# Sparse chunk attention and a gated MLP on one core: six head pairs score mask and data in one 128-row contraction, early bounds in three terms, and a new written order

## The chip, the cores and the metric

The kernel runs on one core of a Trainium2 chip. The metric is the device time of one launch in microseconds (us). A few runs are taken and the median is compared. A separate profiled execution gives the rows that are quoted below; PE is the matrix engine, PEld its weight loads, DVE the vector engine, ACT the scalar engine, POOL the general engine and SP the engine that only issues DMAs here.

## The reference, cut to what matters

There are 4 batches and 8 heads of 768 positions by 64. Keys lie in 24 chunks of 32. Each query keeps the six chunks with the largest upper bound of its score, and attends to these under the causal mask. The output of all heads, 512 wide, goes through a gated MLP with a mixing matrix over positions.

```python
ub = sum(max(q * k_min, q * k_max))          # per query and chunk; -1e9 where the chunk lies ahead
top = argsort(ub)[-6:]
scores = where(selected & causal, q @ k.T / 8, -1e9)
x = softmax(scores) @ v                       # heads side by side: 768 x 512 per batch
h = relu(x @ w_in);  u, w = h[:, :512], h[:, 512:]
w_n = (w - mean(w)) / sqrt(var(w) + 1e-6)
out = (u * (w_spatial @ w_n + b)) @ w_out
```

## The kernel before, in words

**Work items.** Two heads form a pair; there are 16 pairs, four for each batch. Pairs 0 to 3 (batch 0) are worked in two halves of 384 positions, named 0a, 0b and so on; pairs 4 to 15 are whole. Each pair passes through `load`, `prep` and `attend`, and after the four pairs of a batch `mlp` runs. The kernel is not scheduled by its loops. Each call of `op(name, costs, function, reads, writes)` makes a work item, and a table, `ORDER`, lists all the items in one written sequence, with a letter for the engine (P for PE, D, A, G for POOL, S for SP) and digits for the buffers taken. `replay` (L115 on) gives engines and buffers by this table, and each engine runs its items in that order. The numbers in `op` served the search for the table and play no part on the chip.

**prep** (L490 to L628). Queries and keys are cast to 16 bits (`c_k`, `c_q`). For pairs 0 to 9 PE transposes them (`t_k`, `t_q`, L516) and ACT or DVE evicts the result (`e_k`, `e_q`); for pairs 10 to 15 one DMA transpose does both (`x_kq`, L524). DVE reduces each key chunk to maximum and minimum (`kmm`, L530), with the minimum negated, and small copies place them (`km`). `rq0` and `rq1` (L541 to L550) make relu(q) and relu(-q). Two matmuls for each tile of 128 queries (`ub`, L558) then give the bound, relu(q) times maximum plus relu(-q) times negated minimum. `ubm` (L567) adds the causal mask of the diagonal on DVE. `max` (L576, L581) finds the largest eight, `grd` (L590) makes a guard column, `sel` (L602, L605) a 0/1 matrix of chunks that are not selected, three PE transposes (`tsel`, L616) turn it, and `es` evicts it.

**attend** (L630 to L762). For whole pairs the scores lie in three groups of two PSUM tiles, each with seven blocks of 128 by 128 for each head in three or four strips (`WHOLE`). A group is two sets of matmuls. In the first (L658) each strip contracts the 64 rows of one head, and the two heads use the two halves of the array. In the second (L671) each strip contracts 32 rows of `expand` (a chunk's column spread over its 32 keys, times -30000) with the turned selection, and adds the mask. ACT takes the exponential (`exp`, L693), POOL zeroes the upper triangle of diagonal blocks (`tri`, L704), PE multiplies by the values (`av`, L727), DVE normalizes (`rec`, `nrm`), and a DMA or PE transpose (`xx`, `tx`) puts the result where the MLP reads it.

**mlp** (L764 on). For each of six tiles: `v` and `u` projections (L776), relu (`rv`, `ru`, L783, L785), statistics (`bn`, `ag`), `ln` and `rs` for the reciprocal deviation, `vn` (L808) to normalize, `s` (the mixing matrix, L826), `g` (L830), a transpose `xg` (L847), `o` (L855), its eviction `eo`, and the store `so` (L860).

**Order around the change.** PE begins with 22 matmuls on zeros (`w0` to `w3`, L424), 13 of them ahead of the first transpose. SP issues every DMA; an issue that waits holds all that follow it.

Of the kernel before, what the change touches and what calls it, by code (L numbers as in the profile page):

```python
# [14 lines left out]
P = 128  # L15
# [7 lines left out]
XBAR = 1300.0  # L23
# [11 lines left out]
def t_pool(n):  # L35
    return n * 0.9 + 85.0
# [107 lines left out]
RINGS = {"hst": 9, "st": 8, "kqT": 6, "kq16": 2, "x16": 2, "x16d": 2, "e": 7, "vraw": 6, "selT": 5}  # L144
# [17 lines left out]
t_k3aP:3 tsel1aP:2 e_k3aD:3 es1aD:1 kmm0_3aD:0 t_k0bP:0 t_q3aP:1 ub2aP:3 ubm2aD: kmm1_3aD: t_q0bP:2 e_q3aA: max2aD:0
rq1_3aD:1 sel2aD:1 rq0_3aD: e_k0bA: kmm1_0bD:1 preset_vt4G: km1_3aG:4 grd2aG: c_k1bG:2 preset_vt1G: c_q2bG:1 c_v1aG:5
e_q0bA: km0_3aA: sc1a_0P:01 exp1a_01A:1 exp1a_00A: av0aP:1 tsel2aP:0 ub3aP:2 t_k1bP:3 es2aD:2 rq0_1bD:0 ubm3aD:
kmm0_0bD: rq0_0bA:1 rq1_0bA: e_k1bA: max3aD:1 rec0aD:0 km0_0bA: sel3aD:1 nrm0aD:0 kmm0_1bD:2 c_k2bG:0 grd3aG: km1_0bG:
sc2a_0P:10 tsel3aP:0 av1aP:3 ub0bP:2 t_q2bP:1 es3aD:3 rec1aD:1 ubm0bD: kmm1_1bD: max0bD:0 nrm1aD:1 t_k2bP:0 sel0bD:1
c_q3bG:3 c_v2aG:4 km1_1bG: c_q4G:2 grd0bG: c_wv2G:0 c_k3bG:1 c_v3aG:1 exp2a_01A:2 exp2a_00A: rq1_1bA: e_q2bA: km0_1bA:
e_k2bA: sc3a_0P:01 t_q3bP:1 e_q3bD: tx0aP:3 ub1bP:0 tsel0bP:2 es0bD:4 ubm1bD: max1bD:1 tx1aP:1 av2aP:2 rec2aD:2
sel1bD:1 nrm2aD:0 kmm0_2bD:0 exp3a_00A:3 exp3a_01A: sc0b_0P:01 av3aP:0 rec3aD:0 tx2aP:2 nrm3aD:1 ex2aD:0 rq1_3bD:1
rq0_2bA:0 ex0aA: ex1aA: exp0b_01A:4 exp0b_00A: t_k3bP:3 grd1bG: t_q4P:1 tsel1bP:0 tx3aP:2 e_k3bA: ex3aD: c_v0bD:  # L170
c_wv0G: es1bD:0 c_wu2D:0 kmm1_2bD: kmm0_3bD:1 c_wv1G: c_wv3G: ld_wu1S:7 ld_wu3S:1 ld_wo3S:2 ld_ws4S:4 ld_k4S:5
ld_ws3S:6 sc0b_1P:10 exp0b_10A:5 exp0b_11A: e_q4A:4 rq0_3bD: v0_0P:2 v0_2P:3 km0_2bG: c_wu0A: tri0b_00G: sc1b_0P:10
rq1_2bD: rv0_0D:0 exp1b_00A:6 exp1b_01A: c_wu3G: tri0b_10G: km1_2bG: kmm1_3bD: ub2bP:0 ubm2bD: rq1_4D:0 max2bD:0
grd2bD:1 km1_3bG: c_ws4G:0 av0bP:2 rec0bD:1 v0_1P:1 bn0_0D:0 sel2bD: c_wu1G: nrm0bD:0 km0_3bG: c_k4G:3 c_ws3G:1
rv0_2A:1 rv0_1A:2 sc1b_1P:10 ub3bP:3 tsel2bP:0 ubm3bD: es2bD:1 exp1b_10A:0 exp1b_11A: bn0_2D:1 max3bD:1 sel3bD:1
u0_0P:1 t_k4P:2 tws3P:0 ld_ws2S:0 tri1b_00G: c_ws2G:2 grd3bG: ld_k5S:1 ld_v2bS:4 c_v2bD: c_k5G:3 tri1b_10G: ld_q5S:3
ld_k6S:4 ld_v1bS:5 ld_wo2S:7 sc2b_0P:10 e_k4A: ru0_0A:0 exp2b_00A:1 exp2b_01A: ews3D:0 tws2P:3 tsel3bP:2 es3bD:2
bn0_1D:2 kmm1_4D:2 ag0_0D:0 kmm0_4D: rq0_4D: t_k5P:1 u0_2P:0 tx0bP:2 sc2b_1P:10 e_k5A:5 ld_ws5S:5 u0_1P:1 ex0bA:
exp2b_10A:2 exp2b_11A: ld_ws1S:6 ld_k7S:0 c_v1bG: av1bP:2 tri2b_00G: km1_4G:1 epsG:0 km0_4G: tri2b_10G: ag0_2D:
kmm1_5D:0 ru0_1A:1 ews2D: rec1bD:2 kmm0_5D: nrm1bD:1 ru0_2A:2 c_k6G:1 c_q5G:2 sc3b_0P:10 exp3b_00A:3 exp3b_01A: ub4P:3  # L180
tws4P:1 t_q5P:0 av2bP:2 ubm4D: max4D:0 ag0_1D: sel4D:0 rec2bD:0 nrm2bD:0 sc3b_1P:10 ld_v5S:1 ld_v3bS:7 ld_q7S:4
km0_5A:0 km1_5G: e_q5A: exp3b_10A:4 exp3b_11A: c_ws5G:3 grd4G: c_k7G:0 c_ws1G:2 tri3b_00G: tri3b_10G: tx1bP:3 tx2bP:0
ews4D: ex1bD: ex2bD: rq0_5D:1 tws5P:2 tsel4P:1 rq1_5D: es4D:3 tws1P:3 t_k7P:0 ews5D: c_q7D:3 ews1D: e_k7A:0 sc4_0P:10
exp4_01A:5 exp4_00A: ub5P:1 c_wo3G: c_v3bG: av3bP:2 ubm5D: max5D:1 rec3bD:1 nrm3bD:1 sel5D:0 t_k6P:0 grd5G: ld_q6S:3
c_q6G:2 ld_k8S:5 ld_ws0S:0 c_ws0G:0 ld_v4S:6 c_v4G:0 ln0_0A:0 e_k6A:1 rs0_0A: sc4_1P:01 exp4_11A:0 exp4_10A: tx3bP:3
t_q7P:2 t_q6P:0 ex3bD: tsel5P:1 v0_3P:3 sc4_2P:10 e_q6A: rv0_3A:3 e_q7A: exp4_20A:6 exp4_21A: v0_4P:0 u0_3P:3 v0_5P:2
ru0_3A:3 rv0_4A:4 rv0_5A:5 kmm0_7D:1 es5D:4 kmm1_6D:2 vn0_2D:0 bn0_3D:0 vn0_1D:1 kmm0_6D: rq1_6D:0 rq1_7D:1 ag0_3D:1
kmm1_7D: bn0_4D:1 bn0_5D:2 rq0_6D: sc5_0P:10 exp5_00A:1 exp5_01A: c_v5G:5 tri4_00G: ag0_4D: tri4_20G: tri4_10G:
km1_7G:3 km1_6G:4 ld_q8S:2 c_k8G:1 tws0P:1 u0_4P:3 av4_0P:0 av4_1P:2 ld_wo0S:4 c_wo0G: c_q8G:3 ews0A: ld_k9S:3 bcolS:0
ld_k10S:0 c_k9G:2 ld_k11S:6 km0_6G: ld_q12S:1 ld_q10S:5 ag0_5D: vn0_0D:2 ln0_1A:1 rec4_0D:2 nrm4_0D:0 rec4_1D:0  # L190
nrm4_1D: ru0_4A:4 rs0_1A: sc5_1P:10 t_k8P:1 t_q8P:0 ub6P:3 u0_5P:2 exp5_11A:2 exp5_10A: sc5_2P:01 e_k8A:2 vn0_5D:3
vn0_4D:4 c_wo2D: ubm6D: vn0_3D:5 ru0_5A:5 e_q8A: exp5_20A:3 exp5_21A: max6D:0 c_q12G:0 km0_7G: tri5_10G: grd6G:0
c_k10G:1 c_q10G: sel6D: kmm1_8D:0 s0_0P:1 tsel6P:2 s0_1P:3 rq0_7A: es6D:0 kmm0_8D: g0_1D:0 g0_0D: rq1_8D:0 sc6_0P:01
ub7P:0 t_k9P:2 s0_2P:3 exp6_01A:4 exp6_00A: sc6_1P:10 km0_8G:1 preset_snb0G: ld_v6S:4 ld_k12S:2 ubm7D: max7D:1 grd7G:0
tri5_20G: rq0_8D: exp6_11A:0 exp6_10A: km1_8A: g0_2D:1 ld_wo1S:3 x_kq10S:3 e_k9D:4 c_wo1A: sel7D: rq0_10D:1 kmm0_10D:2
tri5_00G: s0_3P:1 av5_1P:3 tsel7P:2 es7A:1 ld_q9S:7 c_q9G:0 c_k11G:1 g0_3D: kmm1_9D:1 sc6_2P:01 exp6_21A:5 exp6_20A:
xg0_1S:0 ld_v8S:1 ld_v9S:0 s0_4P:0 o0_1P:2 eo0_1A:0 sc7_0P:10 exp7_01A:6 preset_km2G: kmm1_10D: rec5_1D:1 nrm5_1D:
# [68 lines left out]
def kernel(  # L266
# [645 lines left out]
```

## Time and profile before

| | us |
|---|---|
| median of 3 runs | 205.67 (204.78 to 205.95) |
| profiled execution, its own time | 205.87 |
| its span in the trace | 204.0 |
| mean granted clock of PE | 0.988 |
| busy: PE, DVE, ACT, POOL | 190.9, 164.5, 145.8, 80.1 |

The span runs from the first to the last instruction of the trace; the profiled execution's own time is 1.87 us longer. Rows of a timeline begin with the start and the length in us. A matmul's length in such a row contains the way through the array, which overlaps the next one; the price of a set of matmuls is therefore read from its start to the start of what follows.

### The profile page before, as it was taken

The page shows a single profiled execution, that of the slowest core. Times are in us where ns is not written, and L with a number is a line of the kernel's source. Part 1 is how long each engine was busy: PE and PEld are TensorE (multiplying, and loading weights), DVE is VectorE, ACT ScalarE, POOL GpSimd, SP SyncE. Part 2 cuts the span into 40 slices and gives each one's busy share as a digit, 9 for nine tenths or more (in the row PEclk, how much of TensorE's full clock was granted, in tenths as well). Part 3 has the DMA queues.
Part 4 walks back from the last instruction along what each step waited for, and adds up shares of the span by engine and source line. Part 5 has one row for each costly group of instructions (what it writes and reads, how often), then busy time and mean ns, then how long its engine had stood idle before and what let it go on. Part 6 is the DMA issues. An engine that isn't in the chain of part 4 may idle for free.

```text
span 204.0 us, 5938 instructions
## 1 busy us (share of the span) xinstructions
PE 190.9 (94%) x2282; PEld 103.3 (51%) x2282; DVE 164.5 (81%) x523; ACT 145.8 (71%) x232; POOL 80.1 (39%) x167
## 2 busy tenths in 40 slices
PE   7899989999998999798999999999999999999991
PEld 2456646576564455454355554544455456444440
DVE  2699999999999999798499896979998418894352
ACT  4689989999999498746797986687884673344221
POOL 5377848785795455631304642101451121000000
PEclk9969999999999999999999999999999999999998
DMA  5999999989999599699999869999200570701844
GB/s 167 278 249 292 287 359 280 319 223 310 275 208 238 92 224 236 142 145 263 236 213 230 155 78 262 148 261 224 40 0 3 132 154 5 204 2 51 206 156 157
DMA packets 86989, 38.28 MB, mean 188 GB/s; under 512 B 74416, under 2 KB 81584, under 8 KB 86960
## 3 DMA queue, kind: packets, MB, share of 16 engines
q1 hardware_dynamic: 86960, 37.89, 79.4%
q8 instruction: 18, 0.29, 0.6%
q14 instruction: 11, 0.09, 0.1%
HBM read 24.38 MB, written 6.29 MB: 150 GB/s over the span
## 4 chain that ended last, share of the span: by engine, by line
PE 59%; DVE 20%; DMA 7%; POOL 7%; issue 4%; ACT 2%; POOLq 0%; DVEq 0%; ACTq 0%
PE gen L776 16%; PE gen L826 11%; PE gen L855 7%; PE gen L727 7%; PE sc L658 6%; DVE kmm L530 5%; PE sc L671 4%; DMA st<-in_q_dram 3%; POOL n L306 3%; DMA late<-late 2%; PE sc L424 2%; DMA out_dram<-late 2%; DVE max L581 2%; DVE vn L808 2%; PE gen L616 2%
## 5 line engine op out<-in xcount | busy, mean ns | idle before, releaser
L693 ACT ACTIVATE e<-sc 128x768 f16<-128x768 f32 (+1 forms) x96 | 83.2, 917 | 23.3 <-PE sc L671 22.4
L704 POOL TENSOR_SCALAR_AFFINE_SELECT e<-e 128x512 f16<-128x512 f16 (+1 forms) x44 | 28.6, 662 | 31.8 <-ACT e L693 30.0
L826 PE MATMUL gen<-vn,wsT 128*128 128x512 f16 x144 | 34.4, 380 | 0.0
L530 DVE TENSOR_REDUCE kmm<-kqT 128x24 f16<-128x768 f16 (+1 forms) x40 | 30.7, 780 | 0.4 <-ACT kqT L304 0.2
L658 PE MATMUL sc<-kqT 64*128 64x128 f16 (+2 forms) x344 | 27.4, 272 | 0.3 <-ACT e L693 0.3
L727 PE MATMUL gen<-vt,e 128*128 128x65 f16 x672 | 24.8, 193 | 0.5 <-DVE selT L306 0.3
L727 PEld LDWEIGHTS <-e 128*128 128x128 f16 x672 | 23.0, 97 | 4.5 <-issue 1.6
L855 PE MATMUL gen<-w_out,late 128*128 128x512 f16 x96 | 23.7, 379 | 1.2 <-DMA late<-late 1.2
L830 DVE SCALAR_TENSOR_TENSOR late<-gen,bcol,u 128x512 f16<-128x512 f32 x24 | 17.7, 745 | 7.8 <-PE gen L826 7.8
L826 PEld LDWEIGHTS <-wsT 128*128 128x128 f16 x144 | 12.9, 98 | 15.7 <-issue 2.6
L671 PE MATMUL sc<-selT,expand 32*128 32x128 f16 (+2 forms) x344 | 19.0, 273 | 0.2 <-DVE selT L306 0.2
L658 PEld LDWEIGHTS <-kqT 64*128 64x128 f16 x344 | 11.8, 94 | 13.5 <-issue 9.8
L304 ACT ACTIVATE kqT<-gen 128x384 f16<-128x384 f16 (+1 forms) x24 | 15.0, 640 | 3.9 <-PE gen L516 3.7
L794 DVE BATCH_NORM_STATS2 stats<-vraw 128x6 f32<-128x512 f32 x24 | 15.8, 679 | 0.8 <-ACT vraw L783 0.8
L783 ACT ACTIVATE vraw<-gen 128x512 f32<-128x512 f32 x19 | 11.0, 607 | 6.7 <-PE gen L776 6.7
L306 POOL COPY km<-kmm 64x48 f16<-64x48 f16 (+1 forms) x27 | 6.6, 248 | 23.3 <-DVE kmm L530 19.6
L304 ACT ACTIVATE late<-gen 128x512 f32<-128x512 f32 (+1 forms) x12 | 7.1, 598 | 11.4 <-PE gen L839 5.3
L306 DVE COPY late<-gen 128x512 f32<-128x512 f32 x14 | 9.4, 687 | 7.1 <-PE gen L855 5.5
L581 DVE MAX8 max<-gen 128x8 f32<-128x20 f32 (+4 forms) x160 | 14.8, 164 | 0.1
L306 POOL CAST n<-st 128x768 f16<-128x768 f32 x17 | 13.9, 832 | 2.1 <-DMA st<-in_q_dram 1.6
L776 PEld LDWEIGHTS <-early 128*128 128x128 f16 x96 | 9.0, 98 | 11.0 <-issue 0.8
L783 ACT ACTIVATE u<-gen 128x512 f16<-128x512 f32 x18 | 10.5, 601 | 5.5 <-PE gen L776 5.5
(102 smaller groups left out, 299.3 us busy)
## 6 DMA issues: line engine op xcount, KB each, us to landing
out_dram<-late SPq DMA_DIRECT2D x24, 256.0 KB, 2.6
st<-in_q_dram SPq DMA_DIRECT2D x12, 384.0 KB, 5.8
st<-in_k_dram SPq DMA_DIRECT2D x12, 384.0 KB, 5.4
st<-in_v_dram SPq DMA_DIRECT2D x12, 384.0 KB, 6.1
st<-in_moe_w_spatial_dram SPq DMA_DIRECT2D x6, 384.0 KB, 5.1
st<-in_moe_w_in_dram SPq DMA_DIRECT2D x8, 256.0 KB, 4.4
early<-in_k_dram SPq DMA_DIRECT2D x8, 192.0 KB, 3.4
early<-in_q_dram SPq DMA_DIRECT2D x8, 192.0 KB, 3.7
```

Of the source, the lines that this page charges most:

```text
L304: e.activation(out=out, in_=in_, func=Act.Copy)
L306: e.tensor_copy(out, in_)
L530: lambda e, m=m, f=f: e.tensor_reduce(kmm.t[:, m, 0:nch], kq.t[:, 0, s0:s0 + ns].rearrange("d (c j) -> d c j", j=CHUNK), axis=AX.X, op=f, ...
L658: e.matmul(sc[z].t[:, a:a + len(qs) * P].rearrange("p (t c) -> p t c", c=P), lhsT=kq.t[r, 0, t * P:(t + 1) * P], rhs=qv[r, qs[0]:qs[-1] + ...
L671: e.matmul(sc[z].t[:, a:a + len(qs) * P], lhsT=expand.t[r, t * P:(t + 1) * P], rhs=selT.t[r].rearrange("p z c -> p (z c)")[:, c0:c0 + len( ...
L693: e.activation(out=e_.t[:, z, :, 0:w], in_=x.t.rearrange("p (h c) -> p h c", h=2)[:, :, 0:w], func=Act.Exp, scale=scale)
L704: e.affine_select(out=d, in_=d, compare_op=Alu.is_ge, fill=0.0, base=0, channel_multiplier=-1, pattern=[[0, 2 * len(zs)], [1, P]])
L727: e.matmul(avv()[:, n, hi, :], lhsT=es[g].t[:, zz, hi, c:c + P], rhs=vt.t[:, t, hi, 0:D + 1], start=(t == 0), stop=(t == qi))
L776: e.matmul(acc.t, lhsT=x.t[:, ko, t * P:(t + 1) * P], rhs=w.t[:, ko, :], start=(ko == 0), stop=(ko == NDO - 1))
L783: e.activation(dst.t, acc.t, func=Act.Relu)
L826: e.matmul(acc.t, lhsT=wsT.t[:, s, t * P:(t + 1) * P], rhs=vn[s].t, start=(s == 0), stop=(s == NQT - 1))
L855: e.matmul(acc.t, lhsT=gT.t[:, a2 * KO + ko, :], rhs=w_out.t[:, ko, :], start=(ko == 0), stop=(ko == KO - 1))
```

## The change

Five things change in the code, and the table is new.

1. **Wide scores** (`WIDE`, pairs 10 to 15). A tile `qs` holds, for each query and head, the 64 query values and 64 further columns, of which 25 carry the selection and the guard. One item (`c_s`) copies the queries in, `sel` and `grd` write straight into it, and one DMA transpose (`xs`) turns all of it. A tile `kw` holds for each head the 64 key rows (two copies, `kw0` and `kw1`) above or below 64 rows of `expand`, which are preset once. A strip is then one matmul over 128 rows for each head, and the second set of matmuls is gone, as are `tsel` and `es` of these pairs.
2. **Bounds in three terms** (`UB3`, pairs 0 to 5). q times maximum, plus relu(-q) times maximum, plus relu(-q) times negated minimum: `rq0` is gone and each tile has one matmul more. In the same pairs one further matmul for each tile (`tri` by `first`) adds the causal mask, and `ubm` is gone.
3. **vn in the form scale and shift**, so that it may also stand on ACT; a small DVE item `sh` makes the shift, eight times.
4. **Places of tiles in SBUF.** A small pad and another sequence of allocation; `qs` of one slot shares memory with the selection tiles of the halves, and `kw` lies in memory that the early loads used.
5. **Costs in the search** (`t_pool`, `XBAR`, the warm matmuls and others), which do not reach the chip.

In the new table 8 of 24 `vn` stand on ACT, 13 instead of 5 `rv` on DVE, 14 instead of 10 `eo` on ACT. Of the warm matmuls 8 instead of 13 stand ahead of the first transposes, 5 just behind them and 9 after the first scores. The first cast of a query half, `c_q0a`, moves from POOL to DVE. The loads of the values of pairs 12 to 15 move behind `xs13`, `xs14` and `xs15` on SP. Six `xs` are new on SP.

```diff
+WIDE = range(10, 16)
+UB3 = range(6)
...
+            if wide and nm == "q":
+                qs = buf("qs")
+                op(f"c_s{tag}", ..., lambda e, nat=nat: copy(e, within(qs.t, 0, D), nat.t if both is None else nat.t[:, 1]), ...)
...
+        if wide:
+            kw = st["kw"] = buf("kw")
+            for hi in range(2):
+                r = slice(hi * D, (hi + 1) * D)
+                op(f"kw{hi}_{tag}", ..., lambda e, hi=hi, r=r: copy(e, kw.t[r, hi], kq.t[r, 0]), ...)
...
-        for m, sign in ((0, 1.0), (1, -1.0)):
+        three = i in UB3
+        for m, sign in ((1, -1.0),) if three else ((0, 1.0), (1, -1.0)):
...
-                for m in range(2):
+                terms = ((kq.t[:, 1, s0:s0 + ns], 0), (rq.t[:, 1], 0), (rq.t[:, 1], 1)) if three else ((rq.t[:, 0], 0), (rq.t[:, 1], 1))
+                for n, (x, m) in enumerate(terms):
...
+                if causal:
+                    e.matmul(ub.t[...], lhsT=tri.t, rhs=first.t, start=False, stop=True)
...
-        op(f"ubm{tag}", {"DVE": 102.0}, go, reads=[ub, cmask], writes=[ub])
+        if not causal:
+            op(f"ubm{tag}", {"DVE": 102.0}, go, reads=[ub, cmask], writes=[ub])
...
+        if wide:
+            qw = st["qw"] = buf("kqT")
+            op(f"xs{tag}", {"SP": XBAR + 200.0},
+               lambda e: e.dma_start_transpose(out=qw.t.rearrange("p n (t c) -> p (n t) c", c=P), in_=qs.t), ...)
+        else:
+            ... (tsel and es as before)
...
+            def go_wide(e, sc=sc, laid=laid):
+                qv = st["qw"].t.rearrange("p n s -> p (n s)").rearrange("p (t h c) -> p h t c", h=2, c=P)
+                for z in range(2):
+                    for s, (t, qs, col) in enumerate(laid[z][0]):
+                        for hi in range(2):
+                            a = hi * BANK + col
+                            e.matmul(sc[z].t[:, a:a + len(qs) * P].rearrange("p (t c) -> p t c", c=P),
+                                     lhsT=st["kw"].t[:, hi, t * P:(t + 1) * P], rhs=qv[:, hi, qs[0]:qs[-1] + 1:step],
+                                     start=(s == 0), stop=True, skip_group_check=True)
...
+                        if e is nc.scalar:
+                            e.activation(vn[t2].t, vraw[t2].t, func=Act.Identity, scale=rstd[h].t[:, 0, r2], bias=rstd[h].t[:, 1, r2])
```

More of the change, by code (lines that the diff above doesn't have):

```diff
@@ L245 @@
+so3_3S: so3_5S: so3_4S:
 """
@@ L353 @@
     ring("tri", 1, [P, P])
+    ring("first", 1, [P, 2, CPT])
     ring("expand", 1, [P, S])
@@ L633, in attend @@
         st = pair[i]
-        kq, vt, selT = st["kq"], st["vt"], st["selT", half]
+        kq, vt, selT = st["kq"], st["vt"], st.get(("selT", half))
+        wide = i in WIDE
         step = 2 if half is None else 1
```

402 lines of the change are left out of this document (236 added, 166 removed).

## The prediction

> **What bounds the kernel now.** I read the page's first part, then busy time by stretch, then the chain of work that ended last, to see which engine the end hangs on where.
>
> ```profile
> span 204.0 us, 5938 instructions
> PE 190.9 (94%) x2282; PEld 103.3 (51%) x2282; DVE 164.5 (81%) x523; ACT 145.8 (71%) x232; POOL 80.1 (39%) x167
> ```
>
> ```profile
> core 0: us, PE busy (x) PEld busy (x) DVE busy (x) ACT busy (x) POOL busy (x), PEclk, DMA share, GB/s
> 0.00:92.00 92.00, 84.20 (x1189) 49.65 (x1189) 82.49 (x303) 76.53 (x122) 58.48 (x129) 0.98 0.98 241
> 92.00:196.00 104.00, 103.02 (x1071) 52.05 (x1072) 79.91 (x217) 67.51 (x108) 21.61 (x38) 1.00 0.67 142
> 196.00:204.00 8.00, 3.71 (x24) 1.62 (x21) 2.15 (x4) 1.79 (x3) 0.00 (x0) 0.90 0.47 172
> ```
>
> ```profile
> 52.01 0.86 DVE kmm L530
> ...
> 53.14 0.86 DVE kmm L530
> 54.00 0.45 DVE vn L808
> 54.45 0.60 DVE stats L794
> ...
> 77.20 6.00 DMA st<-in_q_dram
> ...
> 87.49 5.00 DMA late<-late
> ...
> 173.35 7.77 PE gen L776 x36
> ```
>
> There are two regimes. From 92 to 196 us PE is busy 103.02 of 104 us: every matmul taken out there is worth its full price, and a wait put in there costs its full length. Before 92 us PE is idle for 92 - 84.20 = 7.8 us, the chain runs through DVE from about 42 to 77 us and through two DMAs from there to 92 us; there PE work may be added at less than its price, and DVE work is what counts. After 196 us the last output tiles are evicted and stored; both orders end in the same kinds of items, and I put no change there.
>
> **The change part by part.** The sum is made against the profiled execution, 205.87 us, which lies 0.20 above the median.
>
> *Scores of pairs 10 to 15.* These rows are the timeline of PE in the second regime.
>
> ```profile
> 121.05 0.33 PE L616 MATMUL gen<-ident,sn 128*128 128x128 f16 x3
> 121.22 0.71 PE L727 MATMUL gen<-vt,e 128*128 128x65 f16 x18
> ...
> 128.92 0.56 PE L658 MATMUL sc<-kqT 64*128 64x384 f16 x6
> 129.40 0.40 PE L671 MATMUL sc<-selT,expand 32*128 32x384 f16 x6
> 129.73 1.44 PE L727 MATMUL gen<-vt,e 128*128 128x65 f16 x42
> 131.01 0.46 PE L558 MATMUL gen<-km,rq 128*128 128x48 f16 x12
> 131.32 1.02 PE L855 MATMUL gen<-w_out,late 128*128 128x512 f16 x4
> ```
>
> From start to start a group costs 129.73 - 128.92 = 0.81 us, 0.48 for the data and 0.33 for the mask. The wide form streams seven blocks of 128 columns for each of two heads, 1792 columns. The chain's row of 36 projections gives 7.77 / 36 = 0.216 us for 512 columns of a full 128-row matmul, so 1792 columns are 3.5 x 0.216 = 0.755 us. That saves 0.06 us in each of 18 groups, **-1.0 us**. The three transposes of `tsel` cost 121.22 - 121.05 = 0.17 us, six times: **-1.0 us**. Both stand in the regime where PE never rests. Faster than its columns a group can't be. By the other row at hand, 128 columns in 0.17 / 3 = 57 ns, it would cost 14 x 57 = 0.79 us and the two terms together -1.4; weight loads exposed by 0.11 us in each group would bring the two terms to 0, the upper bound.
>
> A page weighs against this. The Trainium skill, TensorEngine Tiling (Array Packing), Overview, says that a contraction of 64 rows or fewer can run as two row tiles at up to twice the speed, and that one of 32 rows as four. By that the narrow form would cost half of 0.755 for the data and a quarter for the mask, 0.57 us, and the wide form would lose 0.19 us in each group. The rows say 0.81 us for the narrow form, so I go by the rows; the rule returns as a rival.
>
> *Bounds in three terms, causal mask on PE.* Pairs 0 to 5 have 36 tiles, each with two matmuls more, 72 in all. From 131.01 to 131.32 twelve cost 0.31 us, 26 ns each: 72 make 1.9 us of PE, all ahead of 92 us. The 7.8 us of idle PE there can cover them. I take half, **+0.9 us**; if nothing is covered it is +1.9, if all, 0.
>
> What it takes from DVE and ACT, by groups that keep shapes apart:
>
> ```profile
> L567 DVE TENSOR_TENSOR gen<-gen,cmask 128x48 f32<-128x48 f32 x12 | 2.4, 203 | 0.5 <-PE gen L558 0.5
> L546 DVE TENSOR_SCALAR rq<-kqT 128x384 f16<-128x384 f16 x4 | 2.3, 566 | 0.0
> L567 DVE TENSOR_TENSOR gen<-gen,cmask 128x24 f32<-128x24 f32 x8 | 1.4, 180 | 0.7 <-POOL n L306 0.7
> L548 DVE TENSOR_SCALAR rq<-kqT 128x768 f16<-128x768 f16 x10 | 3.6, 369 | 0.0
> L548 DVE TENSOR_SCALAR rq<-kqT 128x384 f16<-128x384 f16 x4 | 1.0, 247 | 0.0
> L306 DVE CAST w_out<-st 128x512 f16<-128x512 f32 x1 | 1.0, 1023 | 0.0
> L306 DVE CAST w_u<-st 128x512 f16<-128x512 f32 x1 | 0.4, 416 | 0.0
> ```
>
> Ten `ubm` (8 of 180 ns, 2 of 203) and six `rq0` (4 of 247, 2 of 369) leave DVE: 1.8 + 1.7 = 3.5 us of row length. The chain shows that neighbours overlap: `kmm` at 53.14 has 0.86 us to the next start, where its row length is longer by some 0.08 us. Sixteen items less 0.08 each leave 2.2 us. Four more `rq0` leave ACT. Against that the table moves eight `rv` to DVE, three of them ahead of 92 us, and some evictions of the halves; a `bn` over the same 512 columns has 0.60 in the chain's row, so 1.8 us come back and more with the evictions. The bounds are -2.2 and +2.0. I take **-0.6 us**, since `vn` and other items leave DVE in the same stretch.
>
> *The order, waits between DVE and POOL.* Two rows above have the same shape and type, L546 and L548 at 128x384, yet one lasts 566 and the other 247 ns; a cast of 128x512 lasts 1023 in one place and 416 in another. The excess, 4 x 0.32 + 0.61, is 1.9 us, and it falls where DVE bounds. An order that has these waits in its sum can avoid them, and it can also meet new ones: `kw` and `c_s` put 8 copies on DVE and 7 on POOL. Bounds -1.9 and +1; I take **-0.8 us**. The Trainium skill, SBUF — State Buffer, SBUF: two separate sides, says that DVE in its fast modes and POOL lock one pair of ports for a whole instruction; the two row pairs agree, and by it copies between SBUF tiles are the exposed ones.
>
> *Six more DMA transposes, and the wait that takes the place of* `tsel` *and* `es`. The DMA rows of `x_kq`, which has the size of `xs`, then those of the two-pair output transpose, then three stretches:
>
> ```profile
> L524 SPq DMA_TRANSPOSE kqT<-kq x6: 1445/1588/2536, 67.6 to 124.6; - x6
> ...
> DMA to landing us min/median/max: 3.8/4.2/4.4
> ```
>
> ```profile
> DMA to landing us min/median/max: 3.7/4.0/6.0
> ```
>
> ```profile
> 92.00:115.00 23.00, 22.46 (x223) 10.89 (x224) 19.29 (x51) 19.02 (x33) 5.83 (x11) 1.00 1.16 234
> 115.00:145.00 30.00, 29.97 (x390) 15.61 (x387) 25.49 (x93) 23.08 (x34) 8.01 (x17) 1.00 0.91 177
> 145.00:160.00 15.00, 14.58 (x187) 7.69 (x186) 13.04 (x30) 10.11 (x17) 5.28 (x8) 1.00 0.11 21
> ```
>
> Each `xs` takes 4.2 us from issue to landing, 1.6 of them the issue, so 2.6 us of the DMA engines. Four (pairs 10 to 13) must land before about 139 us: 10.4 us. If 1.16 is a full share, the stretch 115:145 has 30 x (1 - 0.91 / 1.16) = 6.5 us free. The value loads that move behind `xs13` free more: three of 384 KB at 234 GB/s are 1.7 us each, 5 us. So the transposes fit, with 1 us to spare. Then the latency: in the new table PE has these items between `sel` and the first scores: pair 10, 7.7 us; 11, 18.0; 12, 8.4; 13, 5.8; 14, 12.8; 15, 11.0, by the prices above (pair 13: two score groups, five tiles of four 512-column matmuls at 4 x 0.216: 1.5 + 4.3). What has to happen:
>
> ```profile
> L602 DVE TENSOR_TENSOR sn<-gen,max 128x240 f16<-128x240 f32 x12 | 4.8, 403 | 0.3
> L306 POOL CAST kq<-st 128x768 f16<-128x768 f32 x8 | 6.5, 824 | 4.6 <-DMA st<-in_k_dram 2.8 <-DMA st<-in_q_dram 1.8
> L590 POOL TENSOR_SCALAR sn<-max 128x12 f16<-128x12 f32 x11 | 3.3, 308 | 22.4 <-DVE max L581 16.0 <-DVE mv L797 4.2 <-DVE rec L733 2.2
> ```
>
> `sel` takes 0.4; the guard (0.3) starts when `max` is done but for pair 13 stands on POOL behind a copy of about the cast's 0.8, so the two end some 0.7 after `sel`; then 4.2: 5.3 us. That leaves 0.5. If an `xs` takes 6.0 pair 13 is 1.3 late, and pair 10 is then still in time. Behind a waiting `xs` on SP stand loads of values and stores, which have room at 145:160, share 0.11. I take **+0.8 us** for this; bounds 0 and +4, which is 1.3 for each of three pairs.
>
> *Copies* `c_s`, `kw`, `vn` *on ACT,* `sh`. At nothing: from 92 to 196 us DVE is idle 24, ACT 36 and POOL 82 us by the stretch rows. If `kw` is late its pair's scores wait for it, so its price would be one copy, under 0.9 us, once.
>
> *The start.* The first transposes in the timeline of PE stand behind 13 warm matmuls, though both casts are done before:
>
> ```profile
> 1.25 4.56 PE L424 MATMUL sc<-w_out 128*128 128x512 f16 x13 [1.25 <-DVE w_out L381]
> ...
> 3.98 0.51 POOL L306 CAST n<-early 128x384 f16<-128x384 f32 x1 [0.17 <-DMA early<-in_q_dram]
> ...
> 5.64 0.50 PE L516 MATMUL gen<-ident,n 128*128 128x128 f16 x6
> ```
>
> The second cast ends at 4.49, the transposes start at 5.64. With 8 in place of 13 ahead they could start 1.1 us sooner. The DMA share of 0.98 over the first 92 us says that loads set a pace of their own soon after, and fewer warm matmuls may bring a lower clock. Bounds -1.1 and +1; **-0.5 us**.
>
> The sum: 205.87 - 1.0 - 1.0 + 0.9 - 0.6 - 0.8 + 0.8 - 0.5 = 203.7. Less the 0.20 to the median: **203.5 us**.
>
> **The rivals.**
>
> *More comes free (chance 0.22).* The UB matmuls are all covered (0), DVE gains its 2.2, the waits of 1.9 vanish, no `xs` is late and the start gives 1.1: 205.67 - 2.0 - 2.2 - 1.9 - 1.1 = 198.5; likely somewhere from there to 201.5. For it: the idle 7.8 us of PE in the first regime. Against: the DMA share of 0.98 there.
>
> *Nothing moves (0.14).* The 1.9 us of new PE work before 92 us lie on the path, because the same engines are full in both orders, and they give back the 2.0 of the scores: 205.6.
>
> *The DMA engines become the bound from 92 to 140 us (0.20), the other side.* Its place is the DMA queue ahead of the first wide scores. It decides from the point where `xs` takes longer than 5.8 less 1.1 = 4.7 us at pair 13, 6.6 at pair 10 and 7.3 at pair 12; the longest landing now is 6.0. The 10.4 us of new transposes find 6.5 free if the moved value loads don't help in time, and 3.9 us remain; each PE wait costs in full, and the last stretch of input transposes (`x_kq14`, `x_kq15`) slips with it by the landing's spread, 2 us. 205.67 - 2.0 + 3.9 + 2 - 0.6 = 209.0; from 207 to 211.
>
> *The tiling rule holds for the pairs' true cost (0.04).* If most of a group's 0.81 us is the change of row tiles and stays when the mode changes elsewhere, the wide form loses 0.19 x 18 = 3.4 us instead of gaining 1.0: 203.5 + 4.4 = 207.9. Rows speak against it.
>
> That the change doesn't do what it says is excluded: the changed program holds 132 score matmuls of 128 rows and 212 of 64.
>
> **How the numbers follow.** The forecast (201.5 to 204.6) has 0.40, the others 0.22, 0.14, 0.20 and 0.04. Within 0.5% (about what a measurement of this kernel can tell from no change) is 204.6 to 206.7. Faster: 0.40 + 0.22 = 0.62; same 0.14; slower 0.20 + 0.04 = 0.24. The range leaves out about 0.07 of the free case below and 0.11 of the DMA case above: 199.5 to 208.8. The forecast's own range is 201.5 to 204.6.
>
> **What would show it.** Right: 128-row score groups of about 0.755 us from start to start; PE from 92 us on as full as before and the end of its work 2 us nearer; DMA share above 0.91 in 115:145 with `xs` landing in under 6 us; the first transposes before 5 us. Wrong: PE waiting for a DMA into the transposed queries ahead of a score group; a score group over 0.81 us; PE idle below 92 us by as much as 7.8 us again; DVE rows of the same shape twice as long in many places.

## The result, and the profile after

The changed kernel takes **204.15 us** (median of 7 runs, 203.72 to 204.65) and the kernel before 205.95 us on the same chip (204.78 to 208.85): a ratio of **0.9894**, with a 95% interval of 0.9862 to 0.9926. Ratios and intervals, here and below, leave out runs more than 1.5% above the fastest of their kernel. The 203.5 us of the forecast stood against a base of 205.67, a ratio of 0.9895. The total came out as foretold. The terms behind it did not, and most of what follows is about them.

The head of the page and the first two stretches, now of the changed kernel:

```profile
span 202.1 us, 5830 instructions
PE 188.6 (93%) x2204; PEld 108.7 (54%) x2204; DVE 167.2 (83%) x526; ACT 150.2 (74%) x231; POOL 86.9 (43%) x172
```

```profile
0.00:92.00 92.00, 84.16 (x1247) 51.02 (x1248) 84.92 (x279) 76.14 (x118) 58.84 (x127) 0.98 0.91 246
92.00:196.00 104.00, 102.25 (x950) 56.98 (x949) 80.86 (x246) 73.22 (x113) 28.03 (x46) 1.00 0.75 161
```

PE's sum falls by 2.3 us; that of the first 92 us stays at 84.2 although 1.8 us of work for the bounds came in. PE is idle there for 92 - 84.16 = 7.84 us, as long as before, which the prediction had listed as a sign of being wrong. The second stretch is nearly as full as before (102.25 of 104, before 103.02). The wide groups lie in it, in the timeline of PE:

```profile
117.08 1.02 PE L861 MATMUL gen<-w_u,early 128*128 128x512 f16 x4
117.94 0.92 PE L764 MATMUL sc<-kqT,early 128*128 128x384 f16 x6
118.71 2.75 PE L917 MATMUL gen<-vn,wsT 128*128 128x512 f16 x12
121.30 0.93 PE L764 MATMUL sc<-kqT,early 128*128 128x256 f16 x8
122.06 1.89 PE L946 MATMUL gen<-w_out,late 128*128 128x512 f16 x8
```

A wide group costs 118.71 - 117.94 = 0.77 us, 122.06 - 121.30 = 0.76: not 0.755, but under 0.81. The `xs` transposes land in time; these are the answers for the two `qs` tiles, four transposes from the shared memory and two from a tile of their own:

```profile
DMA to landing us min/median/max: 3.7/4.0/5.0
```

```profile
DMA to landing us min/median/max: 5.2/5.3/5.4
```

No wait of PE for one of them is in the waits. The tightest is pair 13, as the sum had it: its transpose is issued at 134.06, lands 3.7 us later, and its first scores start at 138.74, so 1.0 us is to spare. The DMA engines work as foretold, above 0.91 from 115 to 145 us:

```profile
115.00:145.00 30.00, 29.34 (x282) 17.14 (x279) 27.46 (x85) 24.23 (x35) 12.83 (x22) 1.00 1.00 190
```

What the prediction did not list is in the chain, the longest step ahead of 92 us but for a load:

```profile
16.23 6.69 DMA st<-in_q_dram
...
54.41 3.76 DVE rq L600
```

### The profile page after: what moved, and what is told of

It is laid out like the page before. It is cut to its first block, busy times and chain, and to the rows that moved or that the text cites. A ratio compares the mean times of both kernels' runs of the same rounds, so it can differ in the third digit from the quotient of the medians.

```text
span 202.1 us, 5830 instructions
## 1 busy us (share of the span) xinstructions
PE 188.6 (93%) x2204; PEld 108.7 (54%) x2204; DVE 167.2 (83%) x526; ACT 150.2 (74%) x231; POOL 86.9 (43%) x172
## 4 chain that ended last, share of the span: by engine, by line
PE 59%; DVE 23%; DMA 6%; issue 4%; ACT 3%; POOL 2%; SPq 0%; POOLq 0%; ACTq 0%; DVEq 0%
PE gen L861 15%; PE gen L917 12%; PE gen L946 6%; PE gen L812 6%; DVE kmm L584 5%; PE sc L764 4%; PE sc L729 4%; DMA st<-in_q_dram 3%; DMA early<-x16d 3%; PE sc L742 2%; DVE max L641 2%; PE gen L552 2%; DVE rq L600 2%; DVE stats L879 2%; PE gen L613 2%
## 5 line engine op out<-in xcount | busy, mean ns | idle before, releaser
L778 ACT ACTIVATE e<-sc 128x1024 f16<-128x1024 f32 (+1 forms) x96 | 83.3, 916 | 15.4 <-PE sc L764 8.1
L309 ACT ACTIVATE kqT<-gen 128x384 f16<-128x384 f16 (+1 forms) x20 | 12.8, 656 | 6.9 <-PE gen L552 6.9
L729 PE MATMUL sc<-kqT 64*128 64x128 f16 (+2 forms) x212 | 17.0, 271 | 0.0
L764 PE MATMUL sc<-kqT,early 128*128 128x256 f16 (+2 forms) x132 | 16.7, 268 | 0.0
L311 POOL COPY km<-kmm 64x24 f16<-64x24 f16 (+1 forms) x25 | 5.8, 237 | 22.7 <-DVE kmm L584 14.1
L861 PEld LDWEIGHTS <-early 128*128 128x128 f16 x96 | 8.9, 98 | 11.6 <-DMA early<-x16d 1.1
L552 PE MATMUL gen<-ident,n 128*128 128x128 f16 x120 | 10.9, 227 | 3.8 <-DVE selT L311 2.4
L861 PEld LDWEIGHTS <-xT 128*128 128x128 f16 x96 | 9.0, 100 | 9.8 <-issue 1.8
L946 PEld LDWEIGHTS <-late 128*128 128x128 f16 x96 | 8.7, 97 | 10.0 <-issue 1.2
L764 PEld LDWEIGHTS <-early 128*128 128x128 f16 x132 | 11.1, 98 | 5.3
L861 PE MATMUL gen<-w_u,xT 128*128 128x512 f16 x48 | 12.9, 400 | 0.4 <-DVE qs L662 0.4
```

The source lines that it names most:

```text
L309: e.activation(out=out, in_=in_, func=Act.Copy)
L729: e.matmul(sc[z].t[:, a:a + len(qs) * P].rearrange("p (t c) -> p t c", c=P), lhsT=kq.t[r, 0, t * P:(t + 1) * P], rhs=qv[r, qs[0]:qs[-1] + ...
L764: e.matmul(sc[z].t[:, a:a + len(qs) * P].rearrange("p (t c) -> p t c", c=P), lhsT=st["kw"].t[:, hi, t * P:(t + 1) * P], rhs=qv[:, hi, qs[0 ...
L778: e.activation(out=e_.t[:, z, :, 0:w], in_=x.t.rearrange("p (h c) -> p h c", h=2)[:, :, 0:w], func=Act.Exp, scale=scale)
L861: e.matmul(acc.t, lhsT=x.t[:, ko, t * P:(t + 1) * P], rhs=w.t[:, ko, :], start=(ko == 0), stop=(ko == NDO - 1))
L946: e.matmul(acc.t, lhsT=gT.t[:, a2 * KO + ko, :], rhs=w_out.t[:, ko, :], start=(ko == 0), stop=(ko == KO - 1))
```

## The experiments

All kernels ran with timed rounds beside the kernel before, and ratios are to it. The chips of these runs gave 206.6 to 207.1 us for the kernel before, so ratios are compared, not times; the changed kernel's is 0.9894. One per cent is 2.06 us. The experiments change the written order and, where said, a few lines. Each keeps the whole computation. Their line numbers are some lines below those of the changed kernel, since the table has other line breaks (L597 and L600 are both `rq0`).

### The long row of DVE at 54 us

In the changed kernel DVE and POOL stand like this (timelines of the two engines):

```profile
54.33 3.84 DVE L600 TENSOR_SCALAR rq<-kqT 128x768 f16<-128x768 f16 x1
58.09 0.34 DVE L311 COPY selT<-gen 128x384 f16<-128x384 f16 x1
```

```profile
53.66 1.59 POOL L311 CAST n<-st 128x768 f16<-128x768 f32 x2
55.21 0.61 POOL L311 CAST w_out<-st 128x512 f16<-128x512 f32 x1
55.78 0.63 POOL L789 TENSOR_SCALAR_AFFINE_SELECT e<-e 128x512 f16<-128x512 f16 x1
56.37 0.82 POOL L311 CAST vt<-st 128x768 f16<-128x768 f32 x1
57.13 0.82 POOL L311 CAST kq<-st 128x768 f16<-128x768 f32 x1
57.94 1.50 POOL L789 TENSOR_SCALAR_AFFINE_SELECT e<-e 128x512 f16<-128x512 f16 x2
59.38 0.82 POOL L311 CAST kq<-st 128x768 f16<-128x768 f32 x1
```

An `rq0` of this shape takes 0.35 us where nothing holds it, the next one at 62.41 us for instance. Here it lasts through six POOL instructions that follow each other without a pause, and ends at 58.17, beside the two masks that began at 57.94. These take 1.50 us together, where two of them take 1.22 in a run below; POOL's row goes on behind them. The selection's eviction `es5` stands behind it, and PE behind that (the waits of PE, then two stretches with the granted clock in the third column from the right):

```profile
PE gen L552 <- DVE selT L311: 2.4, 1, 2.4
```

```profile
50.00:58.00 8.00, 6.07 (x74) 3.22 (x71) 7.81 (x10) 7.87 (x12) 4.73 (x9) 1.00 0.79 207
58.00:62.00 4.00, 3.51 (x30) 2.39 (x30) 3.96 (x12) 0.81 (x1) 2.20 (x3) 0.57 1.14 251
```

After 2.4 us without work PE was granted 0.57 of its clock over 4 us. That this lengthens the run isn't shown: three of the seven timed runs of the changed kernel have a mean granted clock of 1.000 and took 204.36 to 204.65 us, and the four at 0.991 or 0.992 took 203.72 to 204.15.

**The relu on ACT.**

```diff
-... rv0_4D:3 bn0_4D:1 rq0_6D: es5D:4 vn0_2D:0 vn0_0A:1 exp4_10A:0 exp4_11A: ...
+... rv0_4D:3 bn0_4D:1 es5D:4 vn0_2D:0 vn0_0A:1 exp4_10A:0 exp4_11A: rq0_6A: ...
```

> One relu of the queries of pair 6 (rq0_6) moves from DVE to ACT; all else as in the changed kernel (204.15 us). Theory: its row of 3.84 us at 54.33 us is a DVE instruction held off by an unbroken row of POOL instructions; on ACT it takes about 0.85 us, PE's idle time of 2.42 us ahead of the first scores of pair 5 goes, and the time falls by 1.5 to 3 us, to 201.2 to 202.7. Rival: the loads set the pace there, or the next DVE instruction takes the wait: 203.7 to 204.6.

0.9836 (0.979 to 0.9882). That is better by 1.2 us, give or take 1.2, so hardly told apart from the changed kernel, and mostly the rival's answer. DVE's timeline:

```profile
53.72 0.34 DVE L308 COPY selT<-gen 128x384 f16<-128x384 f16 x1
53.98 3.66 DVE L898 TENSOR_SCALAR vn<-vraw,rstd 128x512 f16<-128x512 f32 x1
```

The eviction from PSUM (`gen`) passes at once; the next instruction from SBUF to SBUF, `vn`, takes the wait over and ends at 57.64, in a pause of POOL that lasts from 57.35 to 58.07. PE still idles 2.1 us, now for the eviction behind `vn`.

**A pause in POOL's row.** POOL's casts `c_wo2`, `c_v4` and `c_k11` move behind `tri4_10`.

```diff
-... c_k8G:3 c_q9G:0 c_wo2G: tri4_00G: c_v4G:2 ... c_k11G:0 ... tri4_20G: tri4_10G: ...
+... c_k8G:3 c_q9G:0 tri4_00G: ... tri4_20G: tri4_10G: c_wo2G: c_v4G:2 c_k11G:0 ...
```

> On POOL the casts c_wo2, c_v4 and c_k11 go behind the mask of pair 4's third group, so that POOL's unbroken row from 53.2 to 57.9 us ends after its next mask, at about 55.8 us, when it has to wait for an exponential. DVE as in the changed kernel. Theory: DVE's row at 54.33 us ends with POOL's row, 2 us sooner (1.7 us instead of 3.84), and PE's idle time at 56 us falls to below 0.7 us: 0.980 to 0.984 of the kernel before. Rival: the length of the row doesn't follow POOL's row; 3.8 us again, 0.987 to 0.991.

```profile
53.75 1.74 DVE L597 TENSOR_SCALAR rq<-kqT 128x768 f16<-128x768 f16 x1
55.42 0.34 DVE L308 COPY selT<-gen 128x384 f16<-128x384 f16 x1
```

```profile
54.65 0.63 POOL L786 TENSOR_SCALAR_AFFINE_SELECT e<-e 128x512 f16<-128x512 f16 x1
57.36 1.22 POOL L786 TENSOR_SCALAR_AFFINE_SELECT e<-e 128x512 f16<-128x512 f16 x2 [2.08 <-ACT e L775]
```

The row of DVE has the foretold length: it ends at 55.49, just after POOL's last instruction ahead of its pause (55.28). So here the length is set by POOL's row. The time, 0.9862 (0.9817 to 0.9906), is not what was foretold, and within the noise it is the changed kernel's. The moved casts now run at 58.5 to 61.8 us and hold up three other instructions of DVE there, `vn`, `rq0` and a small one of `rstd` (0.77 us, elsewhere 0.15):

```profile
59.25 0.93 DVE L898 TENSOR_SCALAR vn<-vraw,rstd 128x512 f16<-128x512 f32 x1
60.10 0.97 DVE L597 TENSOR_SCALAR rq<-kqT 128x768 f16<-128x768 f16 x1
```

```profile
59.08 0.83 POOL L308 CAST vt<-st 128x768 f16<-128x768 f32 x1
59.85 1.91 POOL L308 CAST kq<-st 128x768 f16<-128x768 f32 x2
```

POOL has no pause here, and still each of the three gets in after about one POOL instruction. So a DVE instruction isn't always held for the whole row; what lets it in wasn't tried. PE waits for the eviction behind the three:

```profile
PE gen L858 <- DVE u L867: 1.8, 1, 1.8
```

**Another order on DVE.** `rq0_6` and `vn0_2` go behind the items that read PSUM; `ub6` goes behind the first scores of pair 5.

```diff
-... rq0_6D: es5D:4 vn0_2D:0 ... rv0_5D:4 ... bn0_3D:0 e_k8D: ub6P:3 t_q9P:0 ... ubm6D: ... sc5_0P:10 ...
+... es5D:4 ... rv0_5D:4 ... bn0_3D:0 e_k8D: vn0_2D:0 rq0_6D: t_q9P:0 ... sc5_0P:10 ub6P:3 ubm6D: ...
```

> On DVE rq0_6 and vn0_2, both from SBUF to SBUF, go behind five instructions that read PSUM or are statistics; ub6 goes behind the first scores of pair 5 on PE. The rest as in the changed kernel. Theory: only instructions between SBUF tiles wait for POOL's row, so those five pass, the long row of DVE (3.84 us, 3.66 with the relu on ACT) is gone, PE's idle time of 2.4 us at 56 us falls below 0.6 us and the time by 2 us or more, to 0.980 of the kernel before or less. Rival: any DVE instruction waits, the long row stays and the time is the changed kernel's, 0.987 to 0.991.

**202.17 us against 207.04, 0.9782 (0.9739 to 0.9825)**, better than both kernels by intervals that don't meet. The same POOL row stands beside it. What reads PSUM or is statistics passes, as these rows show; `vn` and `rq0`, now behind it, take 0.82 and 0.78 us. The clock stays at 1.00:

```profile
53.94 0.34 DVE L308 COPY selT<-gen 128x384 f16<-128x384 f16 x1
54.90 0.69 DVE L867 TENSOR_SCALAR vraw<-gen 128x512 f32<-128x512 f32 x1 [0.62 <-PE gen L858]
55.51 0.69 DVE L876 BATCH_NORM_STATS2 stats<-vraw 128x6 f32<-128x512 f32 x1
56.16 0.96 DVE L308 COPY kqT<-gen 128x768 f16<-128x768 f16 x1
```

```profile
58.00:62.00 4.00, 2.73 (x30) 1.11 (x26) 3.96 (x22) 2.61 (x6) 1.82 (x3) 1.00 1.03 213
```

The theory holds in its sharper form: which instructions wait matters, not how much DVE has to do. PE's wait at 56 us is gone, as expected, but one of 1.1 us came at 59.8 us, for another eviction. The Trainium skill, SBUF — State Buffer, SBUF: two separate sides, says that the two engines lock the shared ports for one whole instruction. The traces show the same two engines and the same kind of DVE instruction, but a wait of 3.84 us that runs across the boundaries of several POOL instructions, none longer than 0.82 us.

### The wide scores alone

```diff
-WIDE = range(10, 16)
+WIDE = ()
...
-... xs12S:4 ... s2_0P:2 sc14_2P:01 xs15S:0 ... nrm12_0D: ... s2_5P:2 ...
+... tsel12P:2 es12D:1 ... s2_0P:2 sc14_2P:01 ... nrm12_0D: ... tsel15P:0 es15A:4 s2_5P:2 ...
```

> The changed kernel's order with the scores of pairs 10 to 15 back in the narrow form (64 rows plus a mask of 32 rows; tsel and es are back, c_s, kw and xs are out). Theory: the wide form saves 0.81 - 0.77 us in each of 18 groups and 0.17 us of tsel six times, all on the path: the time rises by 1.7 us, to 205.9 (205.4 to 206.4). Rival one, the gain of the change is that of the order alone: 203.8 to 204.6. Rival two, narrow groups are the cheaper form: below 203.5.

1.0315 (1.0249 to 1.038), far above what was expected, and partly my own placing: PE waited 1.8 us for the eviction of `tsel12` and 1.7 us for a PSUM tile ahead of `tsel15`. So this run says little. A second one places the two elsewhere (the lines are against the first):

```diff
-... tsel12P:2 es12D:1 ... sc14_1P:01 u2_4P:0 ... tsel15P:0 es15A:4 s2_5P:2 ...
+... exp11_10A: tsel12P:2 es12A:1 ... tsel15P:0 es15D:4 sc14_1P:01 u2_4P:0 ... s2_5P:2 ...
```

> Scores of pairs 10 to 15 narrow as in the run before of that kind, but tsel and es of pairs 12 and 15 placed so that PE has other work while they run (they cost 1.8 and 1.7 us of waiting there). Theory: what is left against the changed kernel (0.989 of the kernel before) is 18 x 0.04 + 6 x 0.17 = 1.7 us and the two transposes' own placing, 0.998 to 1.003 of the kernel before. Rival: the narrow form also loads DVE and the PSUM tiles in the full stretch, and costs over 4 us, above 1.01. Rival two: order alone, 0.987 to 0.991.

1.0098 (1.0054 to 1.0142). Between this and the changed kernel lie 0.0204, or 4.2 us, give or take 1.1: neither the 1.7 of the theory nor the order alone. The page's sum for PE says the same:

```profile
PE 192.9 (93%) x2354; PEld 104.7 (51%) x2354; DVE 164.8 (80%) x518; ACT 149.2 (72%) x231; POOL 77.4 (37%) x162
```

192.9 - 188.6 = 4.3 us. Where it comes from is seen ahead of the group, not in it:

```profile
118.12 1.02 PE L857 MATMUL gen<-w_u,early 128*128 128x512 f16 x4
119.08 0.56 PE L725 MATMUL sc<-kqT 64*128 64x384 f16 x6
...
125.69 0.33 PE L681 MATMUL gen<-ident,sn 128*128 128x128 f16 x3
125.95 0.56 PE L725 MATMUL sc<-kqT 64*128 64x128 f16 x8
```

Four projections take 119.08 - 118.12 = 0.96 us ahead of a narrow group, and 117.94 - 117.08 = 0.86 ahead of a wide one in the rows above. Three transposes take 0.26 ahead of a narrow group, where the prediction's rows had 0.17 ahead of other work. So each narrow group costs 0.10 us more than its own rows show: a matmul over 64 rows starts 0.10 us later behind a full one than the next full one does. The kernel before shows it too, behind the row at 131.32 that the prediction quoted:

```profile
132.28 0.56 PE L658 MATMUL sc<-kqT 64*128 64x256 f16 x8
```

132.28 - 131.32 = 0.96 again. A narrow group costs 0.81 + 0.10, a wide one 0.77: 0.14 in each of 18, or 2.5 us, with 1.0 for `tsel`. That is 3.5 of the 4.2. The Trainium skill, TensorEngine Tiling (Array Packing), Key Properties, says that a change of the tiling mode drains the array; these rows agree, at 0.10 us for each change from 128 to 64 rows.

### The bounds in three terms

Undone in the new order (rq0 and ubm are back, the 72 matmuls gone):

```diff
-UB3 = range(6)
+UB3 = ()
...
-        ub, causal = buf("gen"), half is not None or i in UB3
+        ub, causal = buf("gen"), i in UB3
```

> The changed kernel's order with the bounds of the first six pairs back in two terms and the causal mask of all pairs on DVE (ten rq0 and ten ubm are back, 72 matmuls of 25 ns are out). The sum of the prediction (half of 1.8 us covered, DVE relief 0.6): 203.8, within 0.5 of the changed kernel. Rival one, the PE work lay on the path in full and DVE had room: 202.3. Rival two, DVE's relief is where the gain of the change came from: 206 or more.

1.0097 (1.0054 to 1.0139), 4.2 us slower than the changed kernel, give or take 1.1. By its number that is rival two. Most of the loss stands before 60 us: the wait of 2.4 us for `es5` ends at 58.49 us in the changed kernel and at 62.33 here. The same stretch in this run and in the changed kernel:

```profile
25.00:45.00 20.00, 17.34 (x276) 10.89 (x273) 18.27 (x58) 18.36 (x25) 13.61 (x29) 1.00 0.91 278
```

```profile
25.00:45.00 20.00, 19.68 (x324) 12.33 (x323) 19.56 (x67) 19.23 (x28) 14.62 (x29) 1.00 1.02 333
```

PE gets 2.3 us less done there, some of it the matmuls that were taken out. DVE is less busy too, 18.27 instead of 19.56 of 20 us, so it isn't its sum that costs here. Its `ubm` wait for PE's bounds, 2.2 us in all within the first 50:

```profile
DVE gen L625 <- PE gen L612: 2.2, 4, 1.0
```

So a part of the 4.2 us may be my own placing of the twenty items; a better one wasn't tried. The same part put into the old order, with the narrow scores, is another matter:

```diff
-... w0P:1 e_q0aA:0 rq1_0aA:0 rq0_0aA: ... ub0aP:2 ubm0aD: max0aD:0 ...
+... w0P:1 e_q0aA:0 rq1_0aA:0 ... ub0aP:2 max0aD:0 ...
```

> The order of the kernel before with the bounds of the first six pairs in three terms and the causal mask of the pairs 0 to 5 on PE (72 matmuls of 25 ns more, ten rq0 and ten ubm less), nothing else but sh. The prediction's terms: +0.9 for PE, -0.6 for DVE: 1.000 to 1.003 of the kernel before. Rival one, relief of DVE and ACT in the first 90 us decides: 0.985 to 0.992. Rival two, all of the PE work is on the path: 1.007 or more.

1.0064 (1.0027 to 1.0101), 1.3 us slower than the kernel before, between the forecast and rival two; the eight `sh` are in this run as well. So the three terms have no single price: put into the old order they cost 1.3 us, taken out of the new one they cost 4.2. They move work from DVE to PE; that only an order which uses the room on DVE gets something for it fits both runs, and isn't shown by them.

### The start

```diff
-... w1P:0 w3P:1 t_k0aP:0 t_q0aP:1 w2P:0 ...
+... w1P:0 w3P:1 w2P:0 t_k0aP:0 t_q0aP:1 ...
```

> All 13 warm matmuls stand ahead of the first transposes again, as before the change; all else as in the changed kernel. The prediction's term: 0.5 us slower, 204.7. Rival one, what the sooner start gains is given back to the loads before 25 us: 204.0 to 204.3. Rival two, five more warm matmuls raise the clock early: faster, 203.5.

This is not the start of the kernel before. There 13 warm matmuls stand ahead of the first transposes and nine fill the time from these to the first bounds; here nothing fills it, since the nine stay behind the first scores. The median was 207.8 us against 207.1 of the kernel before, with single runs from 204.2 to 208.6; no interval came of it. So the edit was run again on the reordered kernel.

> The reordered kernel with all 13 warm matmuls ahead of the first transposes. In the first run of that kind PE idled 1.8 us at 6.6 us and the granted clock was half from 9.7 to 16.5 us. Theory: that repeats, and the later start with the slow clock costs 1.5 to 3 us, 0.986 to 0.993 of the kernel before. Rival, the prediction's term alone: 0.5 us, 0.980 to 0.983. Rival two, given back to the loads before 25 us: 0.976 to 0.980.

0.9873 (0.9818 to 0.9928) against 0.9782: 1.9 us slower, give or take 1.4. The profile, of a run of 206.04 us, has what the theory names, the wait of PE at the end of the first row and the clock in the second (in the run before, the half clock lay at 9.1 to 16.0 us, a little sooner than the expectation says):

```profile
9.09 0.17 PE L610 MATMUL gen<-km,kqT 128*128 128x24 f16 x1 [1.81 <-POOL km L308]
```

```profile
10.00:14.00 4.00, 3.52 (x40) 2.20 (x41) 2.60 (x8) 2.31 (x6) 2.99 (x11) 0.57 0.80 219
```

But the 1.9 us are a mean of unlike runs. The two with a mean granted clock of 1.000 took 202.53 and 203.52 us, 0.980 and 0.985 of the kernel before, so 0.5 and 1.4 us above the reordered kernel's ratio; the ten at 0.982 to 0.992 took 204.72 to 206.83. At full clock the later start thus costs not much more than the prediction's 0.5. The other runs are some 3 us longer, more than the 1.7 us that 0.57 over 4 us can cost by itself, and what else differs in them stays open.

### Room for the transposes

```diff
-               lambda e: e.dma_start_transpose(out=qw.t..., in_=qs.t),
+               lambda e: [e.dma_start_transpose(out=qw.t..., in_=qs.t) for _ in range(2)],
```

> The reordered kernel with each of the six transposes xs issued twice, one behind the other, into the same tile. If the transposes fit with room (the forecast's 0.5 to several us for each pair), the second copy, 1.3 to 2.6 us later, is hidden for pairs 11, 12, 14 and 15 and shows a wait of PE of 1 to 2 us at pairs 13 and perhaps 10: 0.982 to 0.992 of the kernel before. Rival, the DMA engines are all but full from 92 to 140 us: each copy costs its 2.6 us, 1.01 or more. Third, room for all: 0.976 to 0.981.

1.0398 (1.0345 to 1.0452), 0.0616 or 12.7 us above the reordered kernel. The waits of PE, then those of SP ahead of an `xs`:

```profile
PE sc L762 <- DMA kqT<-qs: 3.8, 1, 3.8
PE sc L762 <- DMA kqT<-snab: 3.1, 2, 2.6
PE gen L944 <- DMA late<-late: 3.1, 1, 3.1
```

```profile
SPq L671 <- DMA kqT<-snab: 9.2, 4, 2.5
SPq L671 <- DMA kqT<-qs: 6.1, 2, 3.2
```

PE's are 10.0 us, two of them with a stretch of half clock behind them. SP's tell why. Both copies write the same tile, and SP issues the second only when the first has landed: it waits 9.2 + 6.1 = 15.3 us for that and holds all issues behind. The DMA engines are no fuller for it: their share from 115 to 145 us is 0.94, in the reordered kernel 0.97. So this run shows what a held queue costs, not how many transposes the DMA engines have room for. The DMA rival was wrong about the change itself, in which PE waits for no `xs`; how near it came to being right stays open.

### Further moves

```diff
-... vn0_1D:2 rq0_7D: sh0_1D: ru0_4D:3 ... rec4_1D:0 rq1_9D: g0_3D: c_wo1D: c_v5D:1 nrm4_1D: ...
+... sh0_1D: ru0_4D:3 vn0_1D:2 rq0_7D: ... rec4_1D:0 nrm4_1D: rq1_9D: g0_3D: c_wo1D: c_v5D:1 ...
...
-... c_k10D: g0_2D:1 g0_1D: sel7D:0 rq0_8D: grd7D: ... rec13_0D:0 vn2_0D:2 kw1_15D: nrm13_0D:0 ...
+... g0_2D:1 g0_1D: sel7D:0 grd7D: rq0_8D: c_k10D: rq0_9D:1 ... rec13_0D:0 nrm13_0D:0 vn2_0D:2 kw1_15D: ...
```

> The reordered kernel (0.978 of the kernel before) with five further moves on DVE: the eviction of u0_4 ahead of vn0_1 and rq0_7; nrm4_1 right behind its reciprocal; the guard of pair 7, then c_k10 and rq0_9 behind it; nrm13_0 right behind its reciprocal. Theory: PE's waits of 1.14 us at 59.8, 0.43 at 71.4, 0.82 at 76.3 and part of 0.47 us at 152 lie on the path; without them 2 us less, 0.966 to 0.972. Rival: the loads or DVE's sum bind there and the waits come back elsewhere: 0.976 to 0.981.

0.9819 (0.9777 to 0.9861): the rival. PE's waits at 60 and 76 us fell only from 1.14 to 0.97 and from 0.82 to 0.63 us, two of 0.4 came between where there had been one, and DVE waited for an output tile's store that was issued ahead of two transposes:

```profile
94.85 0.69 DVE L308 COPY late<-gen 128x512 f32<-128x512 f32 x1 [1.95 <-DMA out_dram<-late]
```

```diff
-... xg0_5S:0 ld_k14S:4 so0_3S: ...
+... xg0_5S:0 so0_3S: ld_k14S:4 ...
```

> The reordered kernel (0.978 of the kernel before) with the three moves on DVE that shorten PE's waits at 59.8 and 76.3 us and at 152 us (u0_4's eviction, nrm4_1, nrm13_0), without the moves of c_k10, rq0_9 and the guard, and with the store of output tile 3 one load earlier in SP's queue. Theory: in the run with five moves the gain of about 1 us came back as a wait of 1.6 us at 94 us, for a store of an output tile that was issued behind a load and two transposes of 6.6 us; with the store issued first the gain stays: 0.970 to 0.976. Rival: what ends the first regime is the DMA queue at 88 to 95 us, and the wait comes back there again: 0.977 to 0.983.

0.9809 (0.9775 to 0.9842), the rival again. The store's wait is gone and the time is not shorter: from 59.9 to 98 us PE idles 0.97, 0.41, 0.43, 0.63 and 0.63 us in this run, in the reordered kernel 1.14, 0.43, 0.82 and 0.52. DVE is busy 14.82 of 15 us from 60 to 75 us in the reordered kernel, so I read these waits as the rest of a stretch that DVE bounds, where an item moved ahead makes another late. None of the further moves gained on the reordered kernel.

## Why the prediction was right in its total

Each term, in the prediction's words, with what the runs showed; the four measured ones come from different bases and carry 0.8 to 1.4 us each, and the zero for `xs` is read from the waits.

| step | predicted, us | measured, us |
|---|---|---|
| scores and `tsel` | -2.0 | -4.2 |
| bounds on PE, with DVE's relief | +0.9 - 0.6 | +1.3 in the old order |
| waits between DVE and POOL | -0.8 | +2.3 |
| `xs` waits | +0.8 | 0 |
| the start | -0.5 | -1.9 |
| sum | -2.2 | -2.5; the change itself -2.2 |

The sum of the right column meets the change only because the bounds stand in it with the figure of the old order. With the -4.2 us that they are worth against the run in the new order it would be -8.0. So that the two sums agree proves none of the terms, and that the total was met is in part luck.

**Scores.** The mechanism was right, the size half. The step that failed is "from start to start a group costs 0.81": the start of a narrow group is already late, and the time is booked on the item ahead. The group of 0.77 us is the smaller error.

**Bounds.** 24 matmuls of one bound go from 40.77 to 41.37 us, 25 ns each, as priced. That half of it is covered by PE's idle time was too kind: in the old order 1.3 us remained with all relief counted in and the `sh` added, and in the changed kernel PE's idle time ahead of 92 us is 7.84 us again. What the relief is worth by itself no run shows; the two bases differ by more than the step "I take -0.6" could hold.

**Waits between DVE and POOL.** The sign was wrong. The price came from rows of 0.3 to 0.6 us, as if each wait ended with one POOL instruction, and the upper bound of +1 from eight copies. The change brought one wait of 3.84 us, through six. Taking it away gave 2.3 us, give or take 1.1. Whether the old waits, the 1.9 us that the term counts on, are gone was not added up.

**`xs`.** Landings under 6 us and no wait of PE, as listed under "right". The 0.8 us were set aside for a landing of 6.0 us; the longest is 5.4, and pair 13, the tightest in the sum with 0.5 us to spare, has 1.0.

**The start.** First transposes at 4.30 us, before 5 as foretold. The first bounds start at 6.60 us, in the kernel before at 7.94. The prediction feared a lower clock from fewer warm matmuls; in the profiles it is the other way, 0.66 in 10:14 before and 1.00 in the changed kernel. The size of the term stays open: the 1.9 us are those of 13 warm matmuls ahead and none behind, a start that neither kernel has, and in its two runs at full clock they are 0.5 and 1.4.

**The rivals.** "More comes free" would have been nearly right with the stall away: the reordered kernel's ratio is 0.9782, or 201.2 us on the prediction's base and inside its range, by one wait taken away and not by all of its terms. The tiling rival is refuted in this order: narrow is slower by 2%. By the table, the end came where it was foretold through the cancelling of -2.2 on the scores, -1.4 on the start and -0.8 on `xs` against +3.1 on the port waits and +1.0 on the bounds.

Two things stay open. What the new order does with the old arithmetic was tried only part by part, and `vn` on ACT and the places of the tiles were not tried apart. And the 0.7 us between the rows (3.5) and the runs (4.2) of the wide form wasn't traced further; PE's busy time alone is 4.3 us longer in the narrow run's profile, and its waits from 92 us on are longer by 0.9.

## What to carry to other kernels

Price a set of matmuls from the start of the item ahead of it, with the same item ahead of something else beside it: what a change of row tiles costs is booked there. Look in the table for places where DVE works from SBUF to SBUF beside an unbroken row of POOL, and put what reads PSUM first. An edit that moves work between engines has no price by itself; undo it in the new order and do it in the old one, and expect two answers. A run that is to test room in a queue must not add an order of its own, as the second transposes into one tile did.

## What the runs showed of the hardware

- **A DVE instruction from SBUF to SBUF can wait through several POOL instructions in a row.** 3.84 us (`rq0`), 3.66 (`vn` in its place), 1.74 with a pause put into POOL's row; in another row without a pause three of them got in after about one POOL instruction each (0.77 to 0.97 us). Evictions from PSUM of 0.34 to 0.96 us and statistics passed beside such a row.
- **PE's granted clock fell behind some of its waits and not behind others.** After waits of 1.8 to 2.4 us the granted clock was 0.57 over a stretch of 4 us, in the changed kernel at 58 us and at 10 us with 13 warm matmuls. Behind 2.1 us (the relu on ACT), 1.8 us (POOL's pause) and 3.1 us (the transposes issued twice, at 141 us) it stayed at 1.00, and in the kernel before it was 0.66 from 10 to 14 us with no wait over 0.51 us since the first matmul. What decides wasn't tried.
- **A change from 128 to 64 rows costs 0.10 us,** and it shows on the matmul before it: 0.96 instead of 0.86 us for four projections, 0.26 instead of 0.17 for three transposes.
- **A DMA transpose of 128 by 1536 landed in 3.7 to 5.4 us,** in the changed kernel, where the DMA share is 1.00 from 115 to 145 us and PE waits for none of the six.
